# The last chunk of a cross-covariance attention with maxout FFN, computed in two halves of 256 tokens

## Chip, cores and metric

One core of one Trainium2 chip. The metric is the device time of one execution in microseconds (us). The profiled span is about 1.8 us shorter than the time of the same execution.

## The reference, cut to what matters

```python
# q, k, v: 4 x 6144 x 256; w1, w2, w3: 256 x 768; w_out: 768 x 256
a = softmax(normalised(k).T @ normalised(q))        # 256 x 256 for each batch
x = v @ a                                           # 24576 tokens of 256
h = maximum(maximum(x @ w1, x @ w2), x @ w3)        # 24576 x 768
out = h @ w_out                                     # 24576 x 256, fp32
```

The kernel folds `a` into the three weights (`aw[m]`), so that each chunk of 512 tokens costs three products from `v`, the maximum of the three, and one output product.

## The kernel before

Chunk after chunk runs through the same loop. A chunk has six blocks `fc` of 128 hidden columns. Between the blocks stand the output products of the chunk before ("pending"): six matmuls after each of the blocks 1 to 4. PSUM has eight buffers: six for the block products (`ps_h`, two blocks' worth), two for the outputs (`ps_x`).

```python
    def h_block(gi, aw, fc):
        vt = vts[gi]
        ht = hts[gi]
        fsl = slice(fc * P, (fc + 1) * P)
        hp = []
        for m in range(3):
            t = htile(f"h_ps{m}")                                   # one of six PSUM buffers
            for ic in range(CC):                                    # 2 matmuls of 512 columns
                PE.matmul(t.rearrange("p (t n) -> p t n", t=TPC), lhsT=aw[m][:, ic, fsl], rhs=vt[:, :, ic, :], start=(ic == 0), stop=(ic == CC - 1))
            hp.append(t)
        s_mx = mx_pool.tile([P, CHUNK], BF16, name="s_mx")
        ACT.activation(out=s_mx, in_=hp[0], func=AF.Copy)           # L330
        DVE.tensor_tensor(out=s_mx, in0=hp[1], in1=s_mx, op=ALU.max)        # L331
        DVE.tensor_tensor(out=ht[:, fc, :], in0=hp[2], in1=s_mx, op=ALU.max)  # L332
    ...
    def o_last(gi):                                                 # outputs of the last chunk
        ht = hts[gi]
        o_sb = o_pool.tile([P, TPC, d_model], FP32, name="o_sb")
        pss = [xtile("o_ps") for _ in range(TPC // 2)]
        for fcs in (range(FC - 1), (FC - 1,)):                      # the last block's products come last
            for t in range(TPC):
                half = slice((t % 2) * d_model, (t % 2 + 1) * d_model)
                for fc in fcs:
                    PE.matmul(pss[t // 2][:, half], lhsT=ht[:, fc, t * P:(t + 1) * P], rhs=wo_sb[:, fc, :],
                              start=(fc == 0 and t % 2 == 0), stop=(fc == FC - 1), skip_group_check=True)
        ...
        ACT.activation(out=o0, in_=pss[0], func=AF.Copy)
        DVE.tensor_copy(out=o1, in_=pss[1])
        ACT.dma_start(out=dst[:, 0:2, :], in_=o_sb[:, 0:2, :])      # 256 KB
        SP.dma_start(out=dst[:, 2:4, :], in_=o_sb[:, 2:4, :])       # 256 KB
```

Of the kernel before, what the change touches and what calls it, by code (L numbers as in the profile page):

```python
# [11 lines left out]
BF16 = mybir.dt.bfloat16  # L12
FP8 = mybir.dt.float8e4
AF = mybir.ActivationFunctionType
ALU = mybir.AluOpType
# [16 lines left out]
def kernel(  # L32
# [13 lines left out]
    PE = nc.tensor  # L46
    DVE = nc.vector
    ACT = nc.scalar
    POOL = nc.gpsimd
    SP = nc.sync  # L50

    B, N, C = q.shape
    d_ff = moe_w1.shape[1]
    d_model = C
    P = 128
    CC = C // P
    FC = d_ff // P
    CHUNK = 512
    TPC = CHUNK // P
    NG = N // P  # L60
    NCH = N // CHUNK
# [7 lines left out]
    out_r = out.rearrange("(b ch p t) d -> b ch p t d", p=P, t=TPC, ch=NCH)  # L69
# [9 lines left out]
    ht_pool = ctx.enter_context(tc.tile_pool(name="ht", bufs=3))  # L79
    mx_pool = ctx.enter_context(tc.tile_pool(name="mx", bufs=4))  # L80
# [4 lines left out]
    def htile(name):  # L85
        return ps_h.tile([P, 512], FP32, tag="h", name=name)

    def xtile(name, cols=512, dtype=FP32):
        return ps_x.tile([P, cols], dtype, tag="x", name=name)
# [4 lines left out]
    def alloc_qk(b):  # L94
        qk[b] = (qk_pool.tile([P, NG, C], FP8, name="q_sb", tag="q"),
                 qk_pool.tile([P, NG, C], FP8, name="k_sb", tag="k"))

    def load_k(b, g0, w):
        POOL.dma_start(out=qk[b][1][:, g0:g0 + w, :], in_=k_r[b][:, g0:g0 + w, :])  # L99
# [6 lines left out]
    def load_v(gi):  # L106
        if gi >= B * NCH:
            return
        t = v_pool.tile([P, TPC, C], BF16, name="v_sb")
        POOL.dma_start(out=t, in_=v_r[gi // NCH, gi % NCH])  # L110
        v_tiles[gi] = t
# [30 lines left out]
    wo_sb = consts.tile([P, FC, d_model], BF16, name="wo_sb")  # L142
# [15 lines left out]
    def gram(b):  # L158

        qt, kt = qk[b]  # L160
        kk = htile("kk")
        for tp in range(NG // 2):
            tsl = slice(2 * tp, 2 * tp + 2)
            for j in range(CC):
                jsl = slice(j * P, (j + 1) * P)
                PE.matmul(kk[:, jsl], lhsT=kt[:, tsl, jsl], rhs=kt[:, tsl, jsl], start=(tp == 0 and j == 0),  # L166
                          stop=(tp == NG // 2 - 1), perf_mode=DR, skip_group_check=True)
        dkm = sm.tile([P, C], FP32, name="dkm")
        for j in range(CC):
            jsl = slice(j * P, (j + 1) * P)  # L170
            DVE.tensor_tensor(out=dkm[:, jsl], in0=kk[:, jsl], in1=ident, op=ALU.mult)
        ps = [xtile(f"gram{j}") for j in range(CC)]
        for tp in range(NG // 2):
            tsl = slice(2 * tp, 2 * tp + 2)
            last = tp == NG // 2 - 1
            for j in range(CC):
                jsl = slice(j * P, (j + 1) * P)
                PE.matmul(ps[j][:, 0:C], lhsT=qt[:, tsl, jsl], rhs=kt[:, tsl, :],  # L178
                          start=(tp == 0), stop=last, perf_mode=DR, skip_group_check=True)
                PE.matmul(ps[j][:, C:C + P], lhsT=qt[:, tsl, jsl], rhs=qt[:, tsl, jsl],  # L180
                          start=False, stop=last, perf_mode=DR, skip_group_check=True)
            if tp == 11:
                kb_ps = htile("kb_ps")
                PE.matmul(kb_ps[:, :C], lhsT=ones_f, rhs=dkm, start=True, stop=True)
                lnk = sm.tile([P, C], FP32, name="lnk")
                rkb = sm.tile([P, C], FP32, name="rkb")
                ACT.activation(out=lnk, in_=kb_ps[:, :C], func=AF.Ln)
                ACT.activation(out=rkb, in_=lnk, func=AF.Exp, scale=-0.5)
        return ps, rkb
# [72 lines left out]
    def alloc_aw():  # L262
        return [aw_pool.tile([P, CC, d_ff], BF16, name=f"aw{m}_sb", tag=f"aw{m}") for m in range(3)]
# [30 lines left out]
    hts = {}  # L294
# [6 lines left out]
    def v_transpose(gi):  # L301
        if gi >= B * NCH:
            return
        v_sb = v_tiles.pop(gi)
        SP.dma_start_transpose(out=vt_tile(gi), in_=v_sb.rearrange("p t c -> p (t c)"))
# [10 lines left out]
        ACT.activation(out=vt[:, :half, :], in_=ps[:, :half, :], func=AF.Copy)  # L316
        DVE.tensor_copy(out=vt[:, half:, :], in_=ps[:, half:, :])

    def h_block(gi, aw, fc):
        vt = vts[gi]  # L320
        ht = hts[gi]
        fsl = slice(fc * P, (fc + 1) * P)
        hp = []
        for m in range(3):
            t = htile(f"h_ps{m}")
            for ic in range(CC):
                PE.matmul(t.rearrange("p (t n) -> p t n", t=TPC), lhsT=aw[m][:, ic, fsl], rhs=vt[:, :, ic, :], start=(ic == 0), stop=(ic == CC - 1))  # L327
            hp.append(t)
        s_mx = mx_pool.tile([P, CHUNK], BF16, name="s_mx")
        ACT.activation(out=s_mx, in_=hp[0], func=AF.Copy)  # L330
        DVE.tensor_tensor(out=s_mx, in0=hp[1], in1=s_mx, op=ALU.max)  # L331
        DVE.tensor_tensor(out=ht[:, fc, :], in0=hp[2], in1=s_mx, op=ALU.max)  # L332

    def o_steps(gi):

# [18 lines left out]

        return [lambda t=t: step(t) for t in range(TPC)]

    def o_last(gi):

        ht = hts[gi]
        o_sb = o_pool.tile([P, TPC, d_model], FP32, name="o_sb")  # L360
        pss = [xtile("o_ps") for _ in range(TPC // 2)]
        for fcs in (range(FC - 1), (FC - 1,)):
            for t in range(TPC):
                half = slice((t % 2) * d_model, (t % 2 + 1) * d_model)
                for fc in fcs:
                    PE.matmul(pss[t // 2][:, half], lhsT=ht[:, fc, t * P:(t + 1) * P], rhs=wo_sb[:, fc, :],  # L366
                              start=(fc == 0 and t % 2 == 0), stop=(fc == FC - 1), skip_group_check=True)
        dst = out_r[gi // NCH, gi % NCH]
        o0 = o_sb[:, 0:2, :].rearrange("p t d -> p (t d)")
        o1 = o_sb[:, 2:4, :].rearrange("p t d -> p (t d)")  # L370
        ACT.activation(out=o0, in_=pss[0], func=AF.Copy)
        DVE.tensor_copy(out=o1, in_=pss[1])  # L372
        ACT.dma_start(out=dst[:, 0:2, :], in_=o_sb[:, 0:2, :])
        SP.dma_start(out=dst[:, 2:4, :], in_=o_sb[:, 2:4, :])


    ps = gram(0)
# [4 lines left out]
    aw = alloc_aw()  # L382
# [7 lines left out]
    def hold_loads(gi):  # L390

        POOL.tensor_copy(out=guard, in_=vts[gi][:, TPC - 1, CC - 1, P - 1:P])
# [5 lines left out]
    pending = []  # L398
    for b in range(B):
        more = b + 1 < B  # L400
        if more:
            alloc_qk(b + 1)
        for ch in range(NCH):
            gi = b * NCH + ch
            hts[gi] = ht_pool.tile([P, FC, CHUNK], BF16, name="ht_sb")
            load_v(gi + 4)
            v_transpose(gi + 2)
            if gi == 1:
                hold_loads(2)
            if more and 1 <= ch < 9:  # L410
                load_k(b + 1, (ch - 1) * 6, 6)
                load_q(b + 1, (ch - 1) * 6, 6)
            gaps = [[] for _ in range(FC)]
            if ch == 0:
                if b == 0:
                    for fp in range(1, d_ff // FT):
                        gaps[2 * fp - 2].append(lambda fp=fp: aw_part(et, rinv, aw, fp, FT))
                else:
                    gaps[0].append(lambda: aw_part(et, rinv, aw, 1, FH))
            for s, f in enumerate(pending):  # L420
                gaps[s + 1].append(f)
            if more and 3 <= ch < 11:
                g0 = (ch - 3) * 6
                for i, (which, g) in enumerate(((1, g0), (1, g0 + SQW), (0, g0), (0, g0 + SQW))):
                    gaps[(0, 2, 3, 5)[i]].append(lambda which=which, g=g: square_piece(b + 1, which, g))
            if more and ch == 10:
                gaps[5].append(lambda: fold(b + 1))
            if more and ch == NCH - 1:
                st = {}
                gaps[0].append(lambda: st.update(n=norms(b + 1)))  # L430
                gaps[1].append(lambda: st.update(e=exp_t(gs, *st["n"])))
                gaps[4].append(lambda: st.update(r=rowsums(st["e"])))
            for fc in range(FC):
                h_block(gi, aw, fc)
                for f in gaps[fc]:
                    f()
            pending = o_steps(gi)
            if more and ch == NCH - 2:
                gs = gram_kq(b + 1)
            if more and ch == NCH - 1:  # L440
                et, rinv = st["e"], st["r"]
                aw = alloc_aw()
                aw_part(et, rinv, aw, 0, FH)
    o_last(B * NCH - 1)
    keep_order(tc)


# [33 lines left out]
```

## Time and profile before

| | value |
|---|---|
| time, median of the first 3 runs | 576.76 us |
| span of the profiled run | 574.9 us |
| TensorE busy | 555.1 us, 97% |
| VectorE busy | 406.4 us, 71% |
| last matmul ends | 570.43 us |
| last store issued / landed | 571.17 / 573.57 us |

The busy shares say that TensorE paces the kernel. They don't say what the last chunk is worth: that takes the chain of waits and the timeline of the last 13 us, which the prediction below shows. One view more: what the queue that ends the program (SP) waited for after 568 us. The columns are total us, number of waits, longest.

```profile
SPq L374 <- DVE o_sb L372: 3.6, 1, 3.6
SPq L476 <- DMA out_dram<-o_sb: 2.0, 2, 1.4
```

The last store waits for VectorE's copy. Then the closing part (L476) waits 1.4 us for the one store and 0.6 more for the other. So everything after 570.43 us is a chain: copy, issue, landing, closing barrier.

### The profile page before, as it was taken

Reading aid. Unit: us, or ns where it says so; the run is one execution under the profiler, and the core shown is the slowest. Engines: PE = TensorE matmul, PEld = TensorE weight load, DVE = VectorE, ACT = ScalarE, POOL = GpSimd, SP = SyncE. Lnnn points to the kernel's source line nnn. Section 1 sums busy time; section 2 is a strip of 40 time slices with the busy share of each in tenths; the row PEclk is TensorE's granted clock in tenths of the full one; section 3 lists DMA queues with packets and bytes.
Section 4 is the critical chain, followed back from the end, with each engine's and each line's share of the span. In section 5 each row is a group of like instructions: output and inputs, shape, how many; then the busy total and the mean of one; then the engine's idle time right before and its main releaser. Section 6 shows DMA issues by size and latency. Waiting matters only on the chain.

```text
span 574.9 us, 9325 instructions
## 1 busy us (share of the span) xinstructions
PE 555.1 (97%) x3328; PEld 328.5 (57%) x3328; DVE 406.4 (71%) x627; ACT 307.2 (53%) x530; POOL 227.3 (40%) x235
## 2 busy tenths in 40 slices
PE   3789999999999999999999999999999999999996
PEld 3655555555755555555575555555575555555554
DVE  0048777777577777777748777777848778778774
ACT  1034567677454466776735447767646444444442
POOL 4232257776731028777761006777760000000000
PEclk9999999999999999999999999999999999999999
DMA  9998998885598228977378526788535234322111
GB/s 142 107 144 157 130 178 124 157 133 113 102 118 164 59 66 155 133 152 130 75 131 130 114 75 101 157 131 130 125 84 127 66 82 129 74 91 76 56 73 74
DMA packets 75951, 65.62 MB, mean 114 GB/s; under 512 B 52353, under 2 KB 61953, under 8 KB 75905
## 3 DMA queue, kind: packets, MB, share of 16 engines
q0 software_dynamic: 18928, 26.48, 39.1%
q1 hardware_dynamic: 56832, 38.28, 22.9%
q8 instruction: 26, 0.43, 0.3%
q10 hardware_dynamic: 144, 0.26, 0.1%
q14 instruction: 21, 0.16, 0.1%
HBM read 78.64 MB, written 25.17 MB: 181 GB/s over the span
## 4 chain that ended last, share of the span: by engine, by line
PE 93%; DMA 5%; ACT 0%; DVE 0%; issue 0%; POOL 0%; DVEq 0%; POOLq 0%
PE h_ps L327 65%; PE o_ps L346 21%; DMA q_sb<-in_q_dram 4%; PE gram L235 3%; PE ew_ps L282 3%; DMA k_sb<-in_k_dram 2%; PE o_ps L366 0%; PE gram L178 0%; PE n_ps L216 0%; PE n_ps L218 0%; ACT et L246 0%; PE gram L180 0%; DVE o_sb L372 0%; POOL k_sb L99 0%; DVE scr L253 0%
## 5 line engine op out<-in xcount | busy, mean ns | idle before, releaser
L327 PE MATMUL h_ps<-vt_sb,aw_sb 128*128 128x512 bf16 x1728 | 406.6, 379 | 0.0
L331 DVE TENSOR_TENSOR s_mx<-h_ps,s_mx 128x512 bf16<-128x512 f32 x288 | 197.9, 687 | 98.1 <-ACT s_mx L330 97.1
L327 PEld LDWEIGHTS <-aw_sb 128*128 128x128 bf16 x1728 | 168.2, 98 | 163.0 <-DVE aw_sb L288 3.7
L330 ACT ACTIVATE s_mx<-h_ps 128x512 bf16<-128x512 f32 x288 | 171.4, 595 | 130.7 <-PE h_ps L327 130.7
L332 DVE TENSOR_TENSOR ht_sb<-h_ps,s_mx 128x512 bf16<-128x512 f32 x288 | 199.2, 692 | 30.7 <-PE o_ps L346 0.5
L204 POOL TENSOR_TENSOR acc<-acc,sq 128x768 f32<-128x768 f32 x90 | 147.7, 1651 | 70.7 <-ACT sq L198 70.5
L346 PE MATMUL o_ps<-wo_sb,ht_sb 128*128 128x256 bf16 x1128 | 153.9, 273 | 0.0
L346 PEld LDWEIGHTS <-ht_sb 128*128 128x128 bf16 x1128 | 110.4, 98 | 52.9
L349 ACT ACTIVATE o_sb<-o_ps 128x512 f32<-128x512 f32 x94 | 56.1, 597 | 83.1 <-PE o_ps L346 83.1
L110 POOL DMA_DIRECT2D v_sb<-in_v_dram x48 | 26.8, 562 | 88.5 <-DMA vt_sb<-v_sb 86.6
L198 ACT ACTIVATE sq<-q_sb 128x768 bf16<-128x768 fp8e4 x48 | 40.5, 844 | 0.0
L198 ACT ACTIVATE sq<-k_sb 128x768 bf16<-128x768 fp8e4 x48 | 40.1, 835 | 0.0
L201 POOL CAST acc<-sq 128x768 f32<-128x768 bf16 x6 | 4.9, 821 | 64.6 <-ACT sq L198 64.6
L102 POOL DMA_DIRECT2D q_sb<-in_q_dram x32 | 17.7, 555 | 10.7 <-DMA k_sb<-in_k_dram 9.7
L166 PE MATMUL kk<-k_sb 128*128 128x256 fp8e4 x48 | 7.8, 339 | 11.7 <-DVE k_sb L152 5.4
L285 ACT ACTIVATE aw_sb<-ew_ps,rinv 128x384 bf16<-128x384 f32 (+1 forms) x27 | 14.4, 546 | 5.7 <-PE ew_ps L282 4.8
L282 PE MATMUL ew_ps<-w_sb,et 128*128 128x384 bf16 (+1 forms) x108 | 17.1, 308 | 0.0
L235 PE MATMUL gram<-k_sb,q_sb 128*128 128x512 fp8e4 x144 | 16.8, 277 | 0.0
L99 POOL DMA_DIRECT2D k_sb<-in_k_dram x29 | 16.0, 554 | 1.0 <-POOLq L462 0.8
L235 PEld LDWEIGHTS <-q_sb 128*128 128x256 fp8e4 x144 | 15.9, 136 | 0.6
L178 PE MATMUL gram<-k_sb,q_sb 128*128 128x512 fp8e4 x48 | 10.7, 323 | 3.4 <-DMA q_sb<-in_q_dram 3.4
L166 PEld LDWEIGHTS <-k_sb 128*128 128x256 fp8e4 x48 | 6.5, 182 | 12.8 <-DMA k_sb<-in_k_dram 6.3
(52 smaller groups left out, 103.6 us busy)
## 6 DMA issues: line engine op xcount, KB each, us to landing
out_dram<-o_sb SPq DMA_DIRECT2D x47, 512.0 KB, 2.8
v_sb<-in_v_dram POOLq DMA_DIRECT2D x48, 256.0 KB, 3.7
k_sb<-in_k_dram POOLq DMA_DIRECT2D x24, 192.0 KB, 5.3
q_sb<-in_q_dram POOLq DMA_DIRECT2D x24, 192.0 KB, 6.8
k_sb<-in_k_dram POOLq DMA_DIRECT2D x5, 256.0 KB, 10.8
q_sb<-in_q_dram POOLq DMA_DIRECT2D x5, 256.0 KB, 19.4
w_sb<-in_moe_w_dram POOLq DMA_DIRECT2D x9, 128.0 KB, 5.7
kf<-in_k_dram SPq DMA_DIRECT2D x2, 512.0 KB, 4.3
```

Source lines behind the costliest of these rows:

```text
L102: POOL.dma_start(out=qk[b][0][:, g0:g0 + w, :], in_=q_r[b][:, g0:g0 + w, :])
L110: POOL.dma_start(out=t, in_=v_r[gi // NCH, gi % NCH])
L198: ACT.activation(out=sq, in_=src, func=AF.Square)
L204: POOL.tensor_tensor(out=acc, in0=acc, in1=sq, op=ALU.add)
L235: PE.matmul(g[:, j * C:(j + 1) * C], lhsT=qt[:, tsl, j * P:(j + 1) * P], rhs=kt[:, tsl, :], start=(tp == 0 and j == 0), stop=(tp == NG // ...
L282: PE.matmul(ew[:, :w], lhsT=et[:, j, ic * P:(ic + 1) * P], rhs=w_sb[m][:, j, fsl], start=(j == 0), stop=(j == CC - 1))
L327: PE.matmul(t.rearrange("p (t n) -> p t n", t=TPC), lhsT=aw[m][:, ic, fsl], rhs=vt[:, :, ic, :], start=(ic == 0), stop=(ic == CC - 1))
L330: ACT.activation(out=s_mx, in_=hp[0], func=AF.Copy)
L331: DVE.tensor_tensor(out=s_mx, in0=hp[1], in1=s_mx, op=ALU.max)
L332: DVE.tensor_tensor(out=ht[:, fc, :], in0=hp[2], in1=s_mx, op=ALU.max)
L346: PE.matmul(st["ps"][:, half], lhsT=ht[:, fc, t * P:(t + 1) * P], rhs=wo_sb[:, fc, :], start=(fc == 0), stop=(fc == FC - 1))
L349: ACT.activation(out=st["o"][:, t - 1:t + 1, :].rearrange("p t d -> p (t d)"), in_=st["ps"], func=AF.Copy)
```

## The change

Its intent: compute the last chunk in two halves of 256 tokens, send the first half's output while the second is computed, and have only a small output to copy and to store at the end.

```diff
-    def h_block(gi, aw, fc):
+    def h_block(gi, aw, fc, tsl=slice(0, TPC)):
...                                   # the same block over 256 columns
-    def o_last(gi):
+    def last_chunk(gi, aw, pending):
...
+        def products(ps, t0, i, fcs):
+            for fc in fcs:
+                PE.matmul(ps[:, i * d_model:(i + 1) * d_model], lhsT=hts[gi][:, fc, (t0 + i) * P:(t0 + i + 1) * P],
+                          rhs=wo_sb[:, fc, :], start=(fc == 0 and i == 0), stop=(fc == FC - 1),
+                          skip_group_check=True)
+        first = {}
+        def first_half(i):
+            if i == 0:
+                first["ps"] = xtile("o_ps")
+            products(first["ps"], 0, i, range(FC))
+            if i == HT - 1:
+                ACT.activation(out=o_sb[:, 0:HT, :].rearrange("p t d -> p (t d)"), in_=first["ps"], func=AF.Copy)
+                SP.dma_start(out=dst[:, 0:HT, :], in_=o_sb[:, 0:HT, :])
+        for fc in range(FC):
+            h_block(gi, aw, fc, slice(0, HT))
+            if 1 <= fc <= len(pending):
+                pending[fc - 1]()
+        for fc in range(FC):
+            h_block(gi, aw, fc, slice(HT, TPC))
+            if 1 <= fc <= HT:
+                first_half(fc - 1)
+        ps = xtile("o_ps")
+        for fcs in (range(FC - 1), (FC - 1,)):
+            for i in range(HT):
+                products(ps, HT, i, fcs)
+        ACT.activation(out=o_sb[:, HT, :], in_=ps[:, 0:d_model], func=AF.Copy)
+        DVE.tensor_copy(out=o_sb[:, HT + 1, :], in_=ps[:, d_model:2 * d_model])
+        ACT.dma_start(out=dst[:, HT, :], in_=o_sb[:, HT, :])
+        SP.dma_start(out=dst[:, HT + 1, :], in_=o_sb[:, HT + 1, :])
```

In the changed source, the block's lines are L329 (matmul), L333 (ScalarE) and L334, L335 (VectorE); L369 are the output products of the last chunk, L380 the copy of its first half, L395 to L398 the last copies and stores.

More of the change, by code (lines that the diff above doesn't have):

```diff
@@ L317, in v_transpose_pe @@
         DVE.tensor_copy(out=vt[:, half:, :], in_=ps[:, half:, :])
-    def h_block(gi, aw, fc):
+    def h_block(gi, aw, fc, tsl=slice(0, TPC)):
         vt = vts[gi]
-        ht = hts[gi]
+        n = (tsl.stop - tsl.start) * P
+        ht = hts[gi][:, fc, tsl.start * P:tsl.stop * P]
         fsl = slice(fc * P, (fc + 1) * P)
@@ L324, in h_block @@
         for m in range(3):
-            t = htile(f"h_ps{m}")
+            t = htile(f"h_ps{m}")[:, :n]
             for ic in range(CC):
-                PE.matmul(t.rearrange("p (t n) -> p t n", t=TPC), lhsT=aw[m][:, ic, fsl], rhs=vt[:, :, ic, :], start=(ic == 0), stop=(ic == CC - 1))
+                PE.matmul(t.rearrange("p (t n) -> p t n", n=P), lhsT=aw[m][:, ic, fsl], rhs=vt[:, tsl, ic, :],
+                          start=(ic == 0), stop=(ic == CC - 1))
             hp.append(t)
-        s_mx = mx_pool.tile([P, CHUNK], BF16, name="s_mx")
+        s_mx = mx_pool.tile([P, CHUNK], BF16, name="s_mx")[:, :n]
         ACT.activation(out=s_mx, in_=hp[0], func=AF.Copy)
         DVE.tensor_tensor(out=s_mx, in0=hp[1], in1=s_mx, op=ALU.max)
-        DVE.tensor_tensor(out=ht[:, fc, :], in0=hp[2], in1=s_mx, op=ALU.max)
+        DVE.tensor_tensor(out=ht, in0=hp[2], in1=s_mx, op=ALU.max)
     def o_steps(gi):
@@ L355, in o_steps @@
         return [lambda t=t: step(t) for t in range(TPC)]
-    def o_last(gi):
-        ht = hts[gi]
+    def last_chunk(gi, aw, pending):
+        hts[gi] = ht_pool.tile([P, FC, CHUNK], BF16, name="ht_sb")
         o_sb = o_pool.tile([P, TPC, d_model], FP32, name="o_sb")
-        pss = [xtile("o_ps") for _ in range(TPC // 2)]
-        for fcs in (range(FC - 1), (FC - 1,)):
-            for t in range(TPC):
-                half = slice((t % 2) * d_model, (t % 2 + 1) * d_model)
-                for fc in fcs:
-                    PE.matmul(pss[t // 2][:, half], lhsT=ht[:, fc, t * P:(t + 1) * P], rhs=wo_sb[:, fc, :],
-                              start=(fc == 0 and t % 2 == 0), stop=(fc == FC - 1), skip_group_check=True)
-        dst = out_r[gi // NCH, gi % NCH]
-        o0 = o_sb[:, 0:2, :].rearrange("p t d -> p (t d)")
-        o1 = o_sb[:, 2:4, :].rearrange("p t d -> p (t d)")
-        ACT.activation(out=o0, in_=pss[0], func=AF.Copy)
-        DVE.tensor_copy(out=o1, in_=pss[1])
-        ACT.dma_start(out=dst[:, 0:2, :], in_=o_sb[:, 0:2, :])
-        SP.dma_start(out=dst[:, 2:4, :], in_=o_sb[:, 2:4, :])
+        dst = out_r[gi // NCH, gi % NCH]
+        HT = TPC // 2
+        def products(ps, t0, i, fcs):
[20 more added lines that the diff above has]
+        ps = xtile("o_ps")
+        for fcs in (range(FC - 1), (FC - 1,)):
+            for i in range(HT):
[4 more added lines that the diff above has]
+        SP.dma_start(out=dst[:, HT + 1, :], in_=o_sb[:, HT + 1, :])
@@ L404 @@
             gi = b * NCH + ch
+            if gi == B * NCH - 1:
+                last_chunk(gi, aw, pending)
+                break
             hts[gi] = ht_pool.tile([P, FC, CHUNK], BF16, name="ht_sb")
@@ L443 @@
                 aw_part(et, rinv, aw, 0, FH)
-    o_last(B * NCH - 1)
     keep_order(tc)
```

## The prediction

> **What bounds the kernel now.** I read the page first, for the engine that sets the pace. Its first part gives TensorE 97% of the span:
> ```profile
> PE 555.1 (97%) x3328; PEld 328.5 (57%) x3328; DVE 406.4 (71%) x627; ACT 307.2 (53%) x530; POOL 227.3 (40%) x235
> ```
> The change touches only the last chunk of 512 tokens, so I went next to the chain of waits from 545 us on. It is TensorE without a gap up to 570.43 us; only one VectorE copy follows:
> ```profile
> 566.50 1.29 PE h_ps L327 x6
> 567.80 2.63 PE o_ps L366 x24
> 570.43 0.02 issue
> 570.46 0.69 DVE o_sb L372
> ```
> The chain stops at that copy, at 571.15 us of a span of 574.9. The rest is the last stores and the end of the program, so I read the timeline of the last microseconds:
> ```profile
> 566.54 0.60 ACT L349 ACTIVATE o_sb<-o_ps 128x512 f32<-128x512 f32 x1 [0.92 <-PE o_ps L346]
> 567.03 0.59 ACT L330 ACTIVATE s_mx<-h_ps 128x512 bf16<-128x512 f32 x1
> 567.16 0.33 SPq L352 DMA_DIRECT2D out_dram<-o_sb  x1
> 567.42 2.72 PEld L366 LDWEIGHTS <-ht_sb 128*128 128x128 bf16 x24
> 567.63 2.78 PE L366 MATMUL o_ps<-wo_sb,ht_sb 128*128 128x256 bf16 x24
> 567.66 0.69 DVE L331 TENSOR_TENSOR s_mx<-h_ps,s_mx 128x512 bf16<-128x512 f32 x1 [0.52 <-ACT s_mx L330]
> 568.46 0.69 DVE L332 TENSOR_TENSOR ht_sb<-h_ps,s_mx 128x512 bf16<-128x512 f32 x1
> 570.29 0.60 ACT L371 ACTIVATE o_sb<-o_ps 128x512 f32<-128x512 f32 x1 [2.66 <-issue]
> 570.46 0.69 DVE L372 COPY o_sb<-o_ps 128x512 f32<-128x512 f32 x1 [1.31 <-PE o_ps L366]
> 570.91 0.37 ACTq L373 DMA_DIRECT2D out_dram<-o_sb  x1
> 571.17 0.33 SPq L374 DMA_DIRECT2D out_dram<-o_sb  x1
> ```
> Two things to see. The last VectorE result of the chunk is ready at 569.15, while 20 of the 24 output products run; they last until about 569.98, so nothing waits for it. And the two evictions overlap, ScalarE on one PSUM tile, VectorE on another.
>
> The table of DMA issues gives the transfers:
> ```profile
> out_dram<-o_sb SPq DMA_DIRECT2D x47, 512.0 KB, 2.8
> out_dram<-o_sb ACTq DMA_DIRECT2D x1, 256.0 KB, 2.0
> out_dram<-o_sb SPq DMA_DIRECT2D x1, 256.0 KB, 2.4
> ```
> So the last bytes land at 571.17 + 2.40 = 573.57, and the closing barrier takes 574.88 - 573.57 = 1.31 us more. In quarter-microsecond stretches the packets of the two stores (512 KB) ran from about 571.72 to 573.12 at some 400 GB/s: 0.8 us from the first issue to its first packet, 1.4 us of data, 0.45 us from the last packet to landing.
>
> The groups by form give a 256-column instruction of the kind that the change makes:
> ```profile
> L245 DVE TENSOR_TENSOR e_in<-gram,rkb 128x256 f32<-128x256 f32 x8 | 3.0, 416 | 0.0
> L187 ACT ACTIVATE lnk<-kb_ps 128x256 f32<-128x256 f32 x1 | 0.4, 384 | 20.7 <-PE kb_ps L184 20.7
> ```
>
> **What the skill says.** The Trainium skill, "VectorE: DVE Perf Modes", section on the TRN2 errata, gives an fp32 tensor_tensor as (N+151)/0.96 ns: 691 at 512 columns, 424 at 256. The trace agrees: 692 and 416. Halving the columns saves only 40% of the time. "TensorE: Matmul & The Clock Gate", section "Back-to-back issue gap", has N/2.4 + 2.5 ns: 215.8 and 109.2; the trace has 1.29/6 = 215 for 512 columns and 2.63/24 = 109.6 for 256. TensorE loses almost nothing by halving, VectorE does. "PSUM — Partial Sum Buffer", section on bank collisions, says two engines must not access one bank at once, reads against reads included. The changed program obeys: its last two copies read one PSUM tile, and the VectorE copy waits for the ScalarE copy's semaphore. No run shows that wait yet.
>
> **The change, part by part.**
>
> *TensorE work.* 36 products of 512 columns (36 x 215.7 = 7.76 us) become 72 of 256 (72 x 109 = 7.85): +0.08 us. The 48 output products stay 48. The program's order shows 12 of them moved between blocks of the second half, so only 12 instead of 24 stand at the end.
>
> *VectorE pace.* In the trace a dependent pair of maxima starts 0.79 apart (0.69 + 0.10) and the next pair 0.61 later (0.69 - 0.08). With 416 ns that is 0.52 + 0.34 = 0.86 us per block of 256 tokens. TensorE feeds such a block in 6 x 0.109 = 0.65 us where no output products stand between, as in the second half's last three blocks. There VectorE falls behind by 0.2 us a block. Before, a block without output products fed it in 1.29 us against 1.40, a tenth behind, with 2.6 us of cover at the end.
>
> *The last three blocks.* Clock from the first matmul of the fourth block of the second half. Just before it, the first half's output is complete, and ScalarE copies its 512 columns before it takes the block's first product, as at 566.54 above: that timeline's block started at 566.34, the copy 0.20 later, the activation 0.69, VectorE after it. With a 256-column activation (0.38) VectorE starts at 0.69 + 0.38 + 0.05 = 1.12. It ends the fifth block at 1.12 + 0.86 + 0.52 + 0.42 = 2.92 and the sixth at 3.78. TensorE is through the three blocks at 18 x 0.109 = 1.96 and with four products at 2.40. The next product needs the fifth block: 2.92, plus 0.16 for semaphore and weight load (from the weight loads that waited for VectorE near 38.5 us), is 3.08, a stall of 0.68. Six products later, 3.73, it needs the sixth: 3.94, a stall of 0.21. Stalls: 0.89. Two waits for PSUM buffers of 0.06 each may come earlier, when VectorE holds the tiles of two blocks before. TensorE ends later by 0.08 + 0.89 + 0.1 = about 1.05 us.
>
> *Evictions.* Before: from the last matmul to the last issue 0.76 us (570.41 to 571.17). After: 0.09 + 0.38 (ScalarE) + 0.05 + 0.42 (VectorE: 0.69 less 256/0.96 ns) + 0.02 = 0.97, as they are one after the other: +0.21.
>
> *Stores.* The last 128 KB is issued some 0.45 us behind its neighbour of 128 KB, which needs 0.33 us at 400 GB/s, so it travels alone: 0.8 + 0.33 + 0.45 = 1.6 us against 2.40: -0.8, less 0.06 for rows of 1 KB instead of 2 KB (my allowance), say -0.75. The first half's 256 KB leaves four blocks before the end and lands unseen. In the closing waits one fewer follows the last store: -0.03.
>
> Sum: 1.05 + 0.21 - 0.75 - 0.03 = **+0.5 us**, 577.25.
>
> **Rivals.** First, the intended gain: TensorE does not stall. Then 0.08 + 0.21 - 0.78 = -0.5 us, 576.3. For it: 0.42 us instructions that overlap more than I read, or a VectorE that is not late at the fourth block. Against it: the 0.86 us per block comes from 416 ns instructions measured in this trace, and the stall is 0.7 us, more than an error in one latency. Second, VectorE is behind through the whole chunk and the PSUM buffers (six, two blocks' worth) stall TensorE in the first half too: its twelve pairs are 10.3 us in a chunk of 13, so it has slack, but only where output products fill the gaps (six gaps of 0.65 us). Bad luck in all of them would make +1.0 to +1.5 us, 578. Third, the last transfer is not shorter, as the wait is mostly fixed: then +1.2, 578.0; but 1.4 of the 2.40 us shown were data.
>
> **Range and chances.** All rivals lie within 0.3% of 576.76; the change touches 13 us of 575 and can't move 2% (11.5 us) unless something else breaks. I choose 577.25, range 576.2 to 578.2, the low end for the gain intended, the high end for more stalls and a chip that is a little different. Slower than before I hold at three to one. Faster by over 2%: 0.01, within: 0.98, slower by over 2%: 0.01.
>
> **What would show it.** In the profile after, the chain should no longer be all TensorE at the end but pass through the VectorE maxima. TensorE's gaps: about 0.7 and 0.2 us inside the last twelve products. VectorE maxima at 416 to 424 ns, with no idle before the last four. The last VectorE copy starting after the ScalarE copy's end, not beside it. Landing of the last store about 1.6 us after issue. I am wrong if TensorE runs the last twelve products without a gap, or the last store still takes 2.4 us.

## The result, and the profile after

| | before | after |
|---|---|---|
| time, median of 6 runs | 576.80 us | 577.13 us |
| range of the 6 runs | 576.76 to 576.92 | 576.98 to 577.21 |
| span of the profiled run | 574.9 us | 575.4 us |

The ratio is 1.0005, with a 95% interval of 0.9992 to 1.0018. By that interval the two are the same. The six runs of each do not overlap, though, and the traces show where the 0.3 us come from.

First the chain of waits of the kernel after, the counterpart of the four lines in the prediction. Columns: start, duration, what.

```profile
567.33 0.04 ACT o_sb L380
...
567.82 0.39 ACT s_mx L333
...
568.23 0.43 DVE s_mx L334
...
569.10 0.42 DVE s_mx L334
...
569.62 0.43 DVE ht_sb L335
...
570.10 0.83 PE o_ps L369 x6
...
570.96 0.41 PE o_ps L369 x2
```

Before, the chain was TensorE alone up to the last copy. Now from 567.25 to 570.10 us it runs through ScalarE and VectorE: the first half's 512-column copy (L380), the fourth block's activation behind it, then VectorE's maxima without a break. VectorE itself had stood idle for 0.32 us before that block, waiting for ScalarE. TensorE works on beside them, but its last eight products wait. The timeline shows it from TensorE's side, with the wait in the brackets:

```profile
568.23 0.42 DVE L334 TENSOR_TENSOR s_mx<-h_ps,s_mx 128x256 bf16<-128x256 f32 x1 [0.32 <-ACT s_mx L333]
...
569.62 0.42 DVE L335 TENSOR_TENSOR ht_sb<-h_ps,s_mx 128x256 bf16<-128x256 f32 x1
...
570.10 0.55 PEld L369 LDWEIGHTS <-ht_sb 128*128 128x128 bf16 x6 [0.74 <-DVE ht_sb L335]
...
570.48 0.42 DVE L335 TENSOR_TENSOR ht_sb<-h_ps,s_mx 128x256 bf16<-128x256 f32 x1
570.96 0.11 PEld L369 LDWEIGHTS <-ht_sb 128*128 128x128 bf16 x2 [0.31 <-DVE ht_sb L335]
571.39 0.38 ACT L395 ACTIVATE o_sb<-o_ps 128x256 f32<-128x256 f32 x1 [2.20 <-PE o_ps L369]
571.81 0.37 ACTq L397 DMA_DIRECT2D out_dram<-o_sb  x1
571.81 0.42 DVE L396 COPY o_sb<-o_ps 128x256 f32<-128x256 f32 x1 [0.90 <-ACT o_sb L395]
572.26 0.33 SPq L398 DMA_DIRECT2D out_dram<-o_sb  x1
```

The weights of the fifth of the last twelve products are loaded 0.74 us late, those of the eleventh 0.31 us late, each 0.05 to 0.06 us after the maximum that makes them. And the VectorE copy begins when the ScalarE copy ends, where before they overlapped. The groups by form give the durations behind it, and the table of issues the landings:

```profile
L335 DVE TENSOR_TENSOR ht_sb<-h_ps,s_mx 128x256 bf16<-128x256 f32 x12 | 5.1, 425 | 1.2
L334 DVE TENSOR_TENSOR s_mx<-h_ps,s_mx 128x256 bf16<-128x256 f32 x12 | 5.0, 419 | 1.4 <-ACT s_mx L333 1.3
...
out_dram<-o_sb SPq DMA_DIRECT2D x1, 256.0 KB, 2.0
...
out_dram<-o_sb ACTq DMA_DIRECT2D x1, 128.0 KB, 1.9
out_dram<-o_sb SPq DMA_DIRECT2D x1, 128.0 KB, 1.9
```

To compare traces whose first 550 us differ by a few tenths (the time to the last chunk varies from run to run, in one profile below by 1.8 us), I count from one instruction that all of them share, the last 512-column activation of the last chunk but one. It starts at 556.64 us in the timeline of the kernel before and at 556.65 in the one after (in the rows from halves_only on: 556.51, 558.41, 556.43, 556.38, 556.52, 556.47, 556.74, 556.57). Counted from it, in us, with all the experiments below (TensorE's end and the last issue from the timeline or the chain, landing from the table of issues, to 0.1):

| kernel | TensorE ends | last store issued | last store landed | span ends | time, median | before |
|---|---|---|---|---|---|---|
| before | 13.79 | 14.53 | 16.9 | 18.2 | 576.80 | |
| after | 14.72 | 15.61 | 17.5 | 18.8 | 577.13 | 576.80 |
| halves_only | 14.66 | 15.40 | 17.8 | 19.1 | 577.49 | 576.75 |
| vector_relieved | 14.02 | 14.92 | 16.8 | 18.0 | 576.31 | 576.75 |
| two_banks | 14.72 | 15.19 | 17.3 | 18.6 | 576.76 | 576.75 |
| one_last_store | 14.72 | 15.61 | 17.6 | 18.8 | 577.16 | 576.75 |
| after_again | 14.72 | 15.61 | 17.5 | 18.7 | 577.01 | 576.71 |
| gaps_moved | 14.46 | 15.35 | 17.3 | 18.4 | 576.81 | 576.71 |
| repaired | 14.44 | 14.91 | 17.0 | 18.3 | 576.65 | 576.71 |
| tail_four | 13.79 | 14.22 | 16.4 | 17.6 | 576.15 | 576.71 |

So the change made TensorE end 0.93 us later and the way from there to the last issue 0.15 us longer; the landing got 0.5 us shorter. That is +0.6 at the landing, +0.5 at the end of the span.

### The profile page after: what moved, and what is told of

Read it like the earlier page. It is cut to its first block, busy times and chain, and to the rows that moved or that the text cites. A ratio compares the mean times of both kernels' runs of the same rounds, so it can differ in the third digit from the quotient of the medians. Undisturbed runs are those within 1.5% of the kernel's fastest.

```text
span 575.4 us, 9434 instructions
## 1 busy us (share of the span) xinstructions
PE 555.4 (97%) x3363; PEld 331.6 (58%) x3364; DVE 407.8 (71%) x639; ACT 308.4 (54%) x537; POOL 227.3 (39%) x235
## 4 chain that ended last, share of the span: by engine, by line
PE 93%; DMA 5%; DVE 0%; issue 0%; ACT 0%; POOL 0%; DVEq 0%; ACTq 0%; POOLq 0%
PE h_ps L329 65%; PE o_ps L349 21%; DMA q_sb<-in_q_dram 4%; PE gram L235 3%; PE ew_ps L282 3%; DMA k_sb<-in_k_dram 2%; PE o_ps L369 0%; PE gram L178 0%; PE n_ps L216 0%; PE n_ps L218 0%; ACT et L246 0%; DVE s_mx L334 0%; PE gram L180 0%; POOL k_sb L99 0%; DVE scr L253 0%
## 5 line engine op out<-in xcount | busy, mean ns | idle before, releaser
L329 PE MATMUL h_ps<-vt_sb,aw_sb 128*128 128x512 bf16 (+1 forms) x1764 | 407.0, 375 | 0.0
L334 DVE TENSOR_TENSOR s_mx<-h_ps,s_mx 128x512 bf16<-128x512 f32 (+1 forms) x294 | 198.8, 676 | 97.7 <-ACT s_mx L333 96.6
L329 PEld LDWEIGHTS <-aw_sb 128*128 128x128 bf16 x1764 | 171.7, 98 | 160.6 <-DVE aw_sb L288 3.7
L333 ACT ACTIVATE s_mx<-h_ps 128x512 bf16<-128x512 f32 (+1 forms) x294 | 172.3, 586 | 130.5 <-PE h_ps L329 129.5
L335 DVE TENSOR_TENSOR ht_sb<-h_ps,s_mx 128x512 bf16<-128x512 f32 (+1 forms) x294 | 200.3, 681 | 31.4 <-PE o_ps L349 0.5
L235 PE MATMUL gram<-k_sb,q_sb 128*128 128x512 fp8e4 x144 | 16.8, 276 | 0.0
```

The lines of the kernel that those rows point to most:

```text
L235: PE.matmul(g[:, j * C:(j + 1) * C], lhsT=qt[:, tsl, j * P:(j + 1) * P], rhs=kt[:, tsl, :], start=(tp == 0 and j == 0), stop=(tp == NG // ...
L329: PE.matmul(t.rearrange("p (t n) -> p t n", n=P), lhsT=aw[m][:, ic, fsl], rhs=vt[:, tsl, ic, :], start=(ic == 0), stop=(ic == CC - 1))
L335: DVE.tensor_tensor(out=ht, in0=hp[2], in1=s_mx, op=ALU.max)
```

## The experiments

The theory: halved blocks cost VectorE more than half of a whole one (419 to 425 ns against 692), so it needs 0.86 us for a block that TensorE makes in 0.66, and where blocks follow each other without output products TensorE has to wait for it. Apart from that, the two last copies are in a row because they read one PSUM tile. The rivals: the loss is only that too little work is left behind the last block; or the extra matmuls cost TensorE the time; or the order has nothing to do with it, as VectorE's total sets the end. Five rounds each.

Every interval below contains 1, so by the ratios each run is the same as before; the argument rests on the tails of the traces, with the medians beside them. A few executions are over 1 us longer than the rest: two of before (577.83 and 577.97), one of vector_relieved and one of gaps_moved. They move the ratios; the medians hardly feel them.

### halves_only: the blocks in halves, the outputs as before

```diff
...                                   # first_half is removed
-            if 1 <= fc <= HT:
-                first_half(fc - 1)
-        ps = xtile("o_ps")
+        pss = [xtile("o_ps") for _ in range(HT)]
         for fcs in (range(FC - 1), (FC - 1,)):
-            for i in range(HT):
-                products(ps, HT, i, fcs)
...
+            for t in range(TPC):
+                products(pss[t // 2], t - t % 2, t % 2, fcs)
+        # copies of 512 columns and two stores of 256 KB, as in o_last
```

> The last chunk's blocks in halves as in the change, but its outputs as in the kernel before: 24 products at the end, 512-column copies on two engines, two 256 KB stores. My theory (VectorE, at 0.86 us for a block of 256 tokens that TensorE feeds in 0.65, is the bound where no output products stand between): TensorE ends about 1.0 us later than before, now by waits for PSUM buffers inside the second half's blocks (0.15 to 0.28 us each, from the third block on), while the last products, with 1.3 us of cover, wait for nothing; time before +1.0 us. Rival (the change's loss is only the wait of its last 12 products, because it has too little work behind the last block): the 24 products cover it, and the time is before +0.1 us.

Measured: 577.49 us against 576.75, ratio 1.0009 (0.9996 to 1.0021). TensorE ends 0.87 us later than before (1.0 expected), and the median is 0.74 us above before's (1.0 expected). The chain of waits:

```profile
563.17 2.34 PE h_ps L329 x20
565.51 0.42 DVE ht_sb L335
...
565.98 0.81 PE h_ps L329 x6
...
566.83 0.85 PE h_ps L329 x6
...
567.68 0.86 PE h_ps L329 x6
568.53 2.63 PE o_ps L369 x24
```

The first twenty block products take 2.34 us, 0.117 each. Then six of them take 0.81 to 0.86 us: TensorE has taken VectorE's step, 0.86 us a block. The first of these steps begins when a second maximum of VectorE (L335) ends. That TensorE waits for PSUM buffers, of which the program has six for the blocks, is read from the program; the profile puts these waits (0.16 to 0.22 us at the weight loads) under "issue" and names no buffer. The 24 output products then run in 2.63 us without a wait, as before. So the rival falls. The cover behind the last block doesn't save the time, it only moves the wait: into the blocks here, to the last products in the change.

### vector_relieved: less VectorE work in the second half

Its output is wrong, which doesn't matter for the time. The second maximum covers 8 columns only. The matmuls, waits and stores are those of the change.

```diff
+        if tsl.start:
+            DVE.tensor_tensor(out=ht, in0=hp[1], in1=s_mx, op=ALU.max)
+            DVE.tensor_tensor(out=ht[:, 0:8], in0=hp[2][:, 0:8], in1=ht[:, 0:8], op=ALU.max)
+        else:
...                                   # the two maxima as they were
```

> The change with VectorE's second maximum of each block cut to 8 columns in the second half (wrong result on purpose; same matmuls, same waits, same stores). My theory: the two waits of the last products (0.62 and some 0.25 us in the trace of the change) go down to 0.1 to 0.2 in all, TensorE ends 0.7 us earlier than in the change, and the time is the change's -0.7 us, that is before -0.4. Rival (the 36 extra matmuls or weight loads cost TensorE the time): no change from the change's time, before +0.35.

Measured: 576.31 us against 576.75, ratio 0.9988 (0.9975 to 1.0002), relative error 0.06 as intended. One of its five runs, the profiled one, took 578.23, having lost some 1.8 us before the last chunk. Its chain at the end is TensorE again:

```profile
569.00 1.97 PE h_ps L329 x18
570.96 1.47 PE o_ps L373 x12
```

18 block products take 1.97 us, the twelve output products 1.47. Without a wait twelve take 12 x 0.109 = 1.31, so 0.16 us of waiting is left, of 0.83 in the change (0.62 and 0.21, worked out below). TensorE ends 0.70 us earlier than in the change, as the theory had it. The extra matmuls and weight loads are all still there, so they do not cost the time.

### two_banks: the last two results in two PSUM tiles

```diff
-        ps = xtile("o_ps")
+        ps, ps2 = xtile("o_ps"), xtile("o_ps")
...
-        DVE.tensor_copy(out=o_sb[:, HT + 1, :], in_=ps[:, d_model:2 * d_model])
+        DVE.tensor_copy(out=o_sb[:, HT + 1, :], in_=ps2[:, 0:d_model])
```

> The change with the last two products' results in two PSUM tiles, so that the two copies need not follow each other. Theory: the VectorE copy starts within 0.1 us of the ScalarE copy, not after it; the last store is issued 0.4 us earlier after the last matmul (0.5 instead of 0.89); as the two 128 KB stores then travel together, landing takes 0.2 us more (2.1 instead of 1.9); net the change -0.2 us, before +0.15. Rival: the copies stay in a row for another reason, or the data time eats it all: the change's time, before +0.35.

Measured: 576.76 us against 576.75, ratio 0.9996 (0.9984 to 1.0009). The timeline:

```profile
571.06 0.38 ACT L397 ACTIVATE o_sb<-o_ps 128x256 f32<-128x256 f32 x1 [2.09 <-PE o_ps L395]
571.17 0.42 DVE L398 COPY o_sb<-o_ps 128x256 f32<-128x256 f32 x1 [0.49 <-PE o_ps L395]
571.48 0.41 ACTq L399 DMA_DIRECT2D out_dram<-o_sb  x1
571.62 0.33 SPq L400 DMA_DIRECT2D out_dram<-o_sb  x1
```

Both copies now wait for TensorE, each for its own tile, and overlap. TensorE's end is where it was in the change, the last issue 0.42 us earlier, the landing 2.1 instead of 1.9. The span ends 0.2 us earlier, and the median, level with before, lies 0.3 us nearer to it than the change's. The wait was the shared PSUM tile, and it was worth what was expected or a little more.

### one_last_store: 256 KB in one store at the end

```diff
-        ACT.dma_start(out=dst[:, HT, :], in_=o_sb[:, HT, :])
-        SP.dma_start(out=dst[:, HT + 1, :], in_=o_sb[:, HT + 1, :])
+        SP.dma_start(out=dst[:, HT:TPC, :], in_=o_sb[:, HT:TPC, :])
```

> The change with the last 256 KB in one store after both copies instead of two of 128 KB. If the size of the last store sets its landing as I predicted (0.33 us for 128 KB), landing goes from 1.9 to 2.2 us and the time is the change's +0.3, before +0.65. Rival (rows of 1 KB and a fixed part make the small store hardly faster: the 256 KB store of the first half landed in 2.0 us): landing 2.0, the change's +0.1, before +0.45.

Measured: 577.16 us against 576.75, ratio 1.0003 (0.9990 to 1.0015). Both 256 KB stores of this kernel, the first half's and the last, landed in 2.0 us:

```profile
out_dram<-o_sb SPq DMA_DIRECT2D x2, 256.0 KB, 2.0
```

So it is the rival that holds: a 256 KB store alone lands only 0.1 us after one of 128 KB alone. The change's split into two 128 KB stores is worth about a tenth of a microsecond. What shortened the landing from 2.4 to 1.9 is that less was in the queues at once: before, two stores of 256 KB travelled together.

### after_again: the change once more

No edit.

> The change once more, as the reference of this call and for how far its trace repeats: TensorE's end 0.9 us later than in the kernel before when both are counted from the last 512-column activation ahead of the last chunk's own; two waits of the last products on VectorE of 0.74 and 0.31 us at the weight loads; time before +0.35 us.

Measured: 577.01 us against 576.71, ratio 1.0005 (0.9993 to 1.0018). TensorE's end, the last issue and the two waits (0.74 and 0.31) came out as in the first profile to 0.01 us. Differences of a tenth between two tails are thus real, while the whole span, 575.2 here and 575.4 there, wanders by more.

### gaps_moved: the same work, six products elsewhere

```diff
-            if 1 <= fc <= HT:
-                first_half(fc - 1)
+            if fc in (1, 4):
+                first_half((1, 4).index(fc))
```

> The change with nothing altered but the place of the first half's second run of six output products: after the fifth block of the second half, not after the third. Same instructions, same VectorE work. Theory (VectorE falls behind where blocks follow each other without output products): moving the products between the late blocks lets VectorE catch up, the two last waits on it shrink from 1.05 to 0.6 to 0.7 us together, TensorE ends some 0.4 us earlier than in the change; time the change's -0.4, about before. Rival (the last 12 products must wait for VectorE wherever the others stand, as VectorE's total sets the end): the same TensorE end as the change, before +0.35.

Measured: median 576.81 us against 576.71; the ratio, 1.0007 (0.9994 to 1.0020), includes one run of 578.59, the other four lie between 576.69 and 576.91. TensorE ends 0.26 us earlier than in the change. What waited for VectorE, after 565 us (total, number, longest):

```profile
PEld L369 <- DVE ht_sb L335: 0.6, 2, 0.5
PEld L329 <- issue: 0.2, 1, 0.2
```

The two waits of the last products are 0.18 and 0.45, together 0.63 instead of 1.05, inside what was expected; but a weight load of a block product waits 0.16 us, which the change didn't have, so TensorE gains 0.26 and not 0.4. Same instructions, other order, other end: VectorE's total work alone does not set it. The size was a third smaller than expected.

The run does not show that VectorE caught up, though, for the edit moved a second thing: ScalarE's copy of the first half (L380, 0.60 us) goes with the products. In the change it stands before the fourth block's activation, and VectorE waits 0.32 us for ScalarE there. Here it stands before the last block's:

```profile
568.61 0.60 ACT L380 ACTIVATE o_sb<-o_ps 128x512 f32<-128x512 f32 x1 [0.91 <-PE o_ps L369]
...
569.51 0.42 DVE L334 TENSOR_TENSOR s_mx<-h_ps,s_mx 128x256 bf16<-128x256 f32 x1
```

The timeline names no wait of VectorE in the second half any more. Counted from the common instruction, its last maximum starts at 13.57 us instead of 13.83: 0.26 earlier, all that TensorE gains. So the gain can be the copy's place alone; no run moves the products without the copy, and what their place is worth by itself is not shown.

### repaired: both repairs

The edits of two_banks and gaps_moved together.

> The change with both repairs: the last two results in two PSUM tiles, and the output products moved as in gaps_moved. If the two costs are separate, as my theory has it, the gains add: 0.4 from the waits, 0.25 from the copies (0.42 less the data of two stores together), so the change's -0.65, before -0.3 us. If the copies' wait was covered by something else, only -0.4.

Measured: 576.65 us against 576.71, ratio 0.9998 (0.9984 to 1.0011). Against the change that is -0.36 us in the medians; in the tail the last issue comes 0.70 us earlier (0.28 at TensorE's end, 0.42 in the copies), the landing 0.5. In the tail the gains add, as both parts say they should, and the sum is smaller than expected because the first part is. (In the medians gaps_moved gained 0.20 us and two_banks some 0.3; that sum is not reached, but the change's own two medians are 0.12 us apart.) With both repairs the halved chunk is no better than the kernel before.

### tail_four: whole blocks, another end

Built on the kernel before, without any halving.

```diff
-        pss = [xtile("o_ps") for _ in range(TPC // 2)]
...
+        tiles = [xtile("o_ps"), xtile("o_ps"), htile("o_ps_c"), htile("o_ps_d")]
+        def products(t, fcs):
+            for fc in fcs:
+                PE.matmul(tiles[t][:, 0:d_model], lhsT=ht[:, fc, t * P:(t + 1) * P], rhs=wo_sb[:, fc, :],
+                          start=(fc == 0), stop=(fc == FC - 1))
+        for t in range(3):
+            products(t, range(FC - 1))
+        for t in range(3):
+            products(t, (FC - 1,))
+        products(3, range(FC))
...
+        ACT.activation(out=o_sb[:, 0, :], in_=tiles[0][:, 0:d_model], func=AF.Copy)
+        DVE.tensor_copy(out=o_sb[:, 1, :], in_=tiles[1][:, 0:d_model])
+        SP.dma_start(out=dst[:, 0:2, :], in_=o_sb[:, 0:2, :])
+        DVE.tensor_copy(out=o_sb[:, 2, :], in_=tiles[2][:, 0:d_model])
+        SP.dma_start(out=dst[:, 2, :], in_=o_sb[:, 2, :])
+        ACT.activation(out=o_sb[:, 3, :], in_=tiles[3][:, 0:d_model], func=AF.Copy)
+        ACT.dma_start(out=dst[:, 3, :], in_=o_sb[:, 3, :])
```

> The kernel before with blocks of 512 left whole and only the end altered: products ordered so that the first three tiles of 128 tokens are done when the last begins, four PSUM tiles, copies on two engines, stores of 256, 128 and 128 KB. No halving, so no VectorE lag: TensorE ends within 0.1 us of before. The last store is issued about 0.2 us earlier after that than before (ScalarE copy of 256 columns instead of a VectorE copy of 512), and lands in 2.0 us because only its own 128 KB and a rest of the others are in the way; before -0.5 us. Rival (what counts is only that the first half's output leaves early, so halving is needed): before +-0.1.

Measured: 576.15 us against 576.71, ratio 0.9990 (0.9978 to 1.0003). All five runs (576.04 to 576.35) lie below all nine of before (576.50 to 576.89). The timeline of its end:

```profile
569.52 0.82 PE L365 MATMUL o_ps_d<-wo_sb,ht_sb 128*128 128x256 bf16 x6
569.55 0.39 ACT L374 ACTIVATE o_sb<-o_ps 128x256 f32<-128x256 f32 x1 [2.01 <-issue]
...
570.11 0.33 SPq L376 DMA_DIRECT2D out_dram<-o_sb  x1
570.38 0.38 ACT L379 ACTIVATE o_sb<-o_ps_d 128x256 f32<-128x256 f32 x1 [0.44 <-PE o_ps_d L365]
570.53 0.38 SPq L378 DMA_DIRECT2D out_dram<-o_sb  x1
570.79 0.37 ACTq L380 DMA_DIRECT2D out_dram<-o_sb  x1
```

While the last six products run, the first tiles are already being copied; half of the output is issued 0.25 us before TensorE ends, and the last issue follows it by 0.43 us instead of 0.74. TensorE's end, 13.79, is that of before. The last store landed in 2.2 us, not the 2.0 expected: in stretches of 0.2 us the packets of the 512 KB ran without a break from about 570.9 to 572.35. The intent of the change, output sent early and a small last piece, is worth 0.56 us here, without the halving that lost it there. In the tail 0.31 us of it lie between TensorE's end and the last issue (the last copy takes 0.38 us instead of 0.69), and some 0.2 in the landing; whether the early stores or the smaller last copy and store did it in each, this one run does not separate.

## Why the prediction was right

It said +0.5 us, 577.25; 577.13 was measured, inside the range of 576.2 to 578.2, and the direction (slower, held at three to one) came out too. Term by term:

- **TensorE work, +0.08 us.** The block products of the change ran at 0.109 us each (18 in 1.97 us). Right.
- **VectorE pace, 0.86 us a block against 0.65.** The two chain lines of consecutive first maxima, 568.23 and 569.10, are 0.87 apart; TensorE in halves_only fell into steps of 0.85 and 0.86. Right, and shown by halves_only and vector_relieved from two sides.
- **The two stalls of the last products, 0.68 and 0.21.** The first of the twelve starts at 569.04 in the timeline, so the fifth was due at 569.04 + 4 x 0.109 = 569.48; it came at 570.10, 0.62 later. The eleventh was then due at 570.10 + 6 x 0.109 = 570.75 and came at 570.96, 0.21 later. The sum is 0.83, against 0.89. VectorE ended the fifth block 2.96 us after the fourth block's first matmul (567.08), not 2.92, and by the timeline the product started 0.05 us after that and not 0.16. Up to 0.26 us of the stalls may hang on ScalarE's copy before the fourth block (gaps_moved); the prediction's clock has that copy in it.
- **Two waits for PSUM buffers, 0.1 together.** They did not occur in the change: its 18 block products in a row ran in 1.97 us. Waits of this kind, under "issue" in the profile, came in halves_only, and one of 0.16 us in gaps_moved, where as many block products in a row took 2.11 us; why there and not in the change is not shown. TensorE's end was thus +0.93 and not +1.05.
- **Copies, +0.21.** Measured +0.15, from TensorE's end to the last issue (0.89 less 0.74). The mechanism, one tile and therefore one after the other, is shown by two_banks.
- **Stores, -0.75.** Here a size was off: the landing shortened by 0.5 us, from 2.4 to 1.9, and not to 1.6. I had taken 1.4 us of the 2.40 for data and 1.25 us as fixed for a lone store. The runs give 1.9 us for 128 KB alone, 2.0 for 256 KB alone, 2.1 for the last of two of 128 KB together, 2.4 for the last of two of 256 KB. In stretches of 0.1 us the packets of the last 128 KB ran from about 573.10 to 573.55: 0.84 us from issue to first packet, 0.45 of data, 0.6 to landing, where the prediction had 0.8, 0.33 and 0.45. In one_last_store the 256 KB ran from about 572.85 to 573.50: 0.86, 0.65 and 0.5. So a lone small store is mostly time without data, as the third rival of the prediction had it, though that rival expected no shortening at all. Rows of 1 KB (128 KB stores) and of 2 KB (256 KB) were not compared at one size, so the prediction's allowance of 0.06 us for them stays untested.
- **Closing waits, -0.03.** From landing to the end of the span 1.31 us before and about 1.2 after, as far as landing's rounding allows.
- **The skill's formulas.** Neither is stated for just this use, so the trace decides. The one for VectorE is given for an fp32 add, in a section on operands from SBUF; here the maxima read one operand from PSUM, and took 692 and 419 to 425 ns. The one for TensorE is given there for isolated matmuls; for a stream with weight loads, as here, the section states a lower figure at 512 columns, which the 215 ns measured do not bear out.

The overestimate of the store's gain (0.25 us) was met by the overestimates of the two losses (0.12 and 0.06 us), so the sum, 0.5, is nearer to the result than its parts. That much of the hit is luck; the mechanism, VectorE too slow for halved blocks, is not. For the small rest between +0.5 in the spans and +0.3 in the medians no cause is claimed: the span of one kernel varies by as much from run to run.

## What to carry to other kernels

Before work is cut smaller to shorten a tail, look at which engine pays a fixed part for each instruction: here TensorE halved cleanly (215 to 109 ns) and VectorE did not (692 to about 422 ns), so an engine with slack in whole blocks became the bound in halved ones, and more cover at the end only moved the wait into the blocks. Look too at what stands in the slow engine's way: one ScalarE copy before the fourth block kept VectorE waiting 0.32 us. The same aim was reached by ordering the output products so that three quarters are done while the rest still runs, with a PSUM tile for each, and with no block and no product cut. And a store's landing is not bytes over rate: look for what else is in flight.

## What the Trainium skill lacked or had wrong

- "DMA: Bandwidth & Descriptors", section "Anatomy of one DMA": its fit of 2.0 us + bytes / 436e3 (in us) is for the path of GPSIMD; it has none for stores from SP or ACT. From this case's table: 128 KB 1.9 us, 256 KB 2.0, 512 KB 2.8 (median of 47), each from issue to landing; the fit would give 2.3, 2.6 and 3.2, by our estimate.
- "PSUM — Partial Sum Buffer", section on bank collisions: it states the rule but no price for two readers of one tile. Here it was 0.42 us, one copy of 256 columns, and a second tile took it away (two_banks).
- "VectorE: DVE Perf Modes": the durations it gives hold (an estimate of 424 ns by its formula for 256 columns, 419 to 425 measured), but how long after an instruction one that needs its result starts is not in it as a number: here a dependent maximum starts about 0.1 us after the end of the one in front.
- No page that I read gives the time from the end of a VectorE instruction to the weight load that waits for it: 0.05 to 0.06 us here.
